# The second gated stage's down projection by pairs of batches, in seven block products instead of eight

## The chip, the cores and the metric

The kernel runs on one core of a Trainium2 chip. A core has a matrix engine (TensorE, PE in the rows; PEld is its weight load), a vector engine (VectorE, DVE), an activation engine (ScalarE, ACT), GpSimd (POOL) and a queue engine for transfers (SyncE, SP), and 16 DMA engines that all queues share. The metric is the device time of one execution in microseconds. The kernel before took 1463.2 us, the median of three runs (1461.71 to 1463.65).

## The reference

Three stages follow each other on 4608 tokens (8 batches of 576): an attention against 32 learned memory slots, a gated feed-forward layer (512 to 1536 to 512), and an ELU feed-forward layer (512 to 2048 to 512).

```
a = softmax(phi, axis=2);  k_m = a^T k;  v_m = a^T v          # per batch and head
attn = softmax(q k_m^T / 8) v_m                                # x, 4608 x 512
g = x @ w_gate;  val = x @ w_val
x = (g * sigmoid(g) * val) @ w_out                             # moe,  d_ff 1536
h = x @ w_in
out = where(h > 0, h, exp(min(h, 0)) - 1) @ w_out2             # moe2, d_ff 2048
```

The weights are float64, and a product of rounded 32-bit values would not be exact enough: every operand is kept as a high and a low part (`hi`, `lo`), and every product is three matmuls, hi*hi, hi*lo and lo*hi.

## The kernel before, in words

The 1536 hidden units of the gated layer are twelve blocks of 128, called `u`. The first four are computed right behind each batch's attention (the program's first part, to about 320 us); the other eight in a stage of their own (320 to about 763 us), which reads the attention weights `at` of each batch back from DRAM. The ELU layer is the last stage (756 us to the end). This case is about the middle stage.

In the middle stage the loop `for ps in range(2)` takes four `u` at a time, and inside it all eight batches and both halves of 288 tokens. `vw` folds the values of a batch into the gate and value weights, so that a gate tile is `up1` (line 213): six matmuls of 288 columns (L217, L218, L219). `gate1` ends in a SiLU on ScalarE (L238), `val2` in a product on VectorE (L571), which writes hidden values into token windows of 512 columns that do not agree with the batches of 576. When a window of a `u` is full, `split2h` makes its high part on ScalarE (L228) and its low part on VectorE (L230), and `down2` multiplies it by the four output blocks of `w_out`: twelve matmuls of 512 columns (L222 to L224). There are nine windows, eight `u` each: 72 times twelve, 864 matmuls. After four `u` ScalarE empties the four accumulators (L590), and a GpSimd DMA adds them to `p1d`, the layer's output in DRAM (L591).

Beside this runs `conv`, background work in small portions: the float64 weights are fetched (`wr`), split into words on ScalarE and VectorE (lines 114 to 119 and 132), and for the sixteen weight sets of the last stage `set_split` (L174) also makes the sums of weight blocks that the seven-product method needs, splits them and stores them (`upd`, `dnd`). The last stage already uses seven products for its pairs of token blocks; its first block of 512 tokens, the plain block, is done with eight.

The order of instructions on each engine is fixed when the program is built: a scheduler places them by its own estimate of times, by priorities (`tc.high_priority`) and by `tc.issue_after`. Each engine then takes its list in order. The pools (`wa`, `wo`, `hs` and so on) have a fixed number of buffers; a writer waits for the reader of the buffer's last content.

```
def split2h():
    w, u = chunks.pop(0)
    ready.append((w, u, split_h(hs_p, hw.pop((w, u)), T)))
def down(ps, w, hs, ms, start, stop):
    mm(ps, lhsT=w[0][:, ms], rhs=hs[0], start=start, stop=False)
    mm(ps, lhsT=w[1][:, ms], rhs=hs[0], start=False, stop=False)
    mm(ps, lhsT=w[0][:, ms], rhs=hs[1], start=False, stop=stop)
```

Of the kernel before, what the change touches and what calls it, by code (L numbers as in the profile page):

```python
# [29 lines left out]
NWA = 14  # L30
NWB = 4
# [6 lines left out]
def attention_moe_moe(ctx: ExitStack, tc: tile.TileContext, qT, phiT, kv, kv4, w1g, w1o, w2, out):  # L38
# [8 lines left out]
    wa_p = ctx.enter_context(tc.tile_pool(name="wa", bufs=NWA))  # L47
    st_l = ctx.enter_context(ExitStack())
    wr_p = st_l.enter_context(tc.tile_pool(name="wr", bufs=2))
    wt_p = st_l.enter_context(tc.tile_pool(name="wt", bufs=2))  # L50
    vx_p = st_l.enter_context(tc.tile_pool(name="vx", bufs=4))
    vt_p = st_l.enter_context(tc.tile_pool(name="vt", bufs=B))
# [7 lines left out]
    io_p = st_r.enter_context(tc.tile_pool(name="io", bufs=2, side="right"))  # L60
# [15 lines left out]
    up_d = [dram.tile([128, 8, 2, 256], F32, name=f"upd{q}") for q in range(NQD)]  # L76
    dn_d = [dram.tile([128, 8, 4, 2, 256], F32, name=f"dnd{h}") for h in range(2)]
# [86 lines left out]
    def store_w2():  # L164
        while stores:
            dst, w = stores.pop(0)
            nc.scalar.dma_start(out=dst, in_=w)

    def set_load(kind, q):
        t = SET[kind, q] = uq_p.tile([128, 8, 256], F32, tag="uq", name="uq")  # L170
        load_w(t[:, 2:6].rearrange("p r c -> p (r c)"), fetch_w(w2[q, :, int(kind == "down")]))

    def set_split(kind, q):
        t = SET.pop((kind, q))  # L174
        with later():
            tt(out=t[:, 0:7:6], in0=t[:, 4:6], in1=t[:, 2:5:2], op=ALU.subtract)
            tt(out=t[:, 1], in0=t[:, 5], in1=t[:, 0], op=ALU.subtract)
            tt(out=t[:, 7], in0=t[:, 3], in1=t[:, 1], op=ALU.subtract)
            for r in (0, 4):
                w = up_p.tile([128, 4, 2, 256], F32R, tag="u", name="uw")  # L180
                act(out=w[:, :, 0], in_=t[:, r:r + 4], func=AF.Copy)
                tt(out=w[:, :, 1], in0=t[:, r:r + 4], in1=w[:, :, 0].bitcast(F32), op=ALU.subtract)
                if kind == "up":
                    stores.append((up_d[q][:, r:r + 4], w.bitcast(F32)))
                else:
                    stores.append((dn_d[q // 4][:, r:r + 4, q % 4].rearrange("p r i c -> p r (i c)"),
                                   w.rearrange("p r i c -> p r (i c)").bitcast(F32)))
# [7 lines left out]
    def vw(b, p, pools):  # L195
        t = VW[b, p] = vx_p.tile([128, 2, 2, 512], F32R, tag="vx", name="vw")
        ps = [pool.tile([128, 512], F32, tag=tag, name="pvw") for pool, tag in pools]
# [23 lines left out]
    def down(ps, w, hs, ms, start, stop):  # L221
        mm(ps, lhsT=w[0][:, ms], rhs=hs[0], start=start, stop=False)  # L222
        mm(ps, lhsT=w[1][:, ms], rhs=hs[0], start=False, stop=False)  # L223
        mm(ps, lhsT=w[0][:, ms], rhs=hs[1], start=False, stop=stop)  # L224
# [255 lines left out]

    PD = [(ps_gv, "g")] * 2
    prev = []
    for b in range(B):
# [3 lines left out]
        if b == 0:  # L487
            wo = [lambda u=u: load_wo(u, wa_p) for u in range(UA // 2)]
# [3 lines left out]
        if 4 <= b <= 5:  # L492
            bk += [lambda: load_wg(2, b - 4, wa_p)]
        if b == B - 2:
            wb_p = st_l.enter_context(tc.tile_pool(name="wb", bufs=NWB))
# [6 lines left out]
            fr += [lambda: load_wg(3, 0, wa_p)]  # L502
        if b == B - 1:
            fr += [lambda: load_wg(3, 1, wa_p)]
            fr.append(lambda: load2(0))
            fr += [lambda: load_wo(2, wb_p)]
            fr += [lambda: vw(0, 2, G2)]
            fr += [lambda: load_wo(3, wb_p)]
            fr += [lambda: vw(0, 3, G2)]
# [44 lines left out]
    ps_acc = st_p2.enter_context(tc.tile_pool(name="ps_acc", bufs=1, space=PSUM))  # L554
    st_r = ExitStack()
    hs_p = st_r.enter_context(tc.tile_pool(name="hs", bufs=2, side="right"))
    p1_p = st_r.enter_context(tc.tile_pool(name="p1", bufs=1, side="right"))
    hw_p = st_r.enter_context(tc.tile_pool(name="hw", bufs=2 * UA, side="right"))
    t_p = st_r.enter_context(tc.tile_pool(name="t2", bufs=2, side="right"))
    up_p = st_l.enter_context(tc.tile_pool(name="up", bufs=3))  # L560
    uq_p = st_l.enter_context(tc.tile_pool(name="uq", bufs=1))

    hw, accs, chunks, ready = {}, {}, [], []

    def val2(b, hf, u, s):
        pv = ps_gv.tile([128, HS], F32, tag="g", name="pv")
        up1(pv, VW[b, u // 2], 256 * (u % 2) + 128, at2[b], HS * hf)
        for w, o, c0, c in windows(S * b + HS * hf, HS):
            if o == 0:
                hw[w, u] = hw_p.tile([128, T], F32, tag="h", name="h")  # L570
            last["h"] = stt(out=hw[w, u][:, o:o + c], in0=s[:, c0:c0 + c], scalar=1.0, in1=pv[:, c0:c0 + c],  # L571
                            op0=ALU.mult, op1=ALU.mult)
            if o + c == T:
                chunks.append((w, u))

    def split2h():
        w, u = chunks.pop(0)
        ready.append((w, u, split_h(hs_p, hw.pop((w, u)), T)))

    def down2():  # L580
        w, u, hs = ready.pop(0)
        first, last_u = u % UA == 0, u % UA == UA - 1
        if first:
            accs[w] = [ps_acc.tile([128, T], F32, tag=f"acc{m}", name=f"acc{m}") for m in range(KD)]
        for m in range(KD):
            down(accs[w][m], WO[u], hs, slice(128 * m, 128 * m + 128), first, last_u)
        if last_u:
            p1 = p1_p.tile([128, KD, T], F32, tag="p1", name="p1a")
            for m, acc in enumerate(accs.pop(w)):
                act(out=p1[:, m, :], in_=acc, func=AF.Copy)  # L590
            nc.gpsimd.dma_start(out=p1_d[w], in_=p1, accum_op=ALU.add)  # L591

    def turn():
        if chunks:
            split2h()
        if len(ready) > 1 or ready and not chunks:
            down2()
# [5 lines left out]
    def split_x(k):  # L603
        w = wa_p.tile([128, 2, T], F32R, tag="w", name="xs")
        with later(), tc.issue_after(last["gate"].ins):
# [6 lines left out]
    conv = [lambda p=p, k=k: load_wg(p, k, wa_p) for p in (4, 5) for k in range(2)] + \  # L612
        [lambda u=u: load_wo(u, wa_p) for u in (4, 5)] + \
        [lambda f=f, a=a: f(*a) for kind in ("up", "down") for q in range(NQD)
         for f, a in ((set_load, (kind, q)), (set_split, (kind, q)))]
    vwq = []
    slot, NCONV = 0, len(conv)
    for ps in range(2):
        for b in range(B):
            nb, np_ = (b + 1, ps) if b + 1 < B else (0, ps + 1)  # L620
            for hf in range(2):
                if hf == 0 and np_ < 2:
                    load2(nb)
                for u in range(UA * (ps + 1), UA * (ps + 2)):
                    s = gate1(b, u, at2[b], HS * hf, True)
                    val2(b, hf, u, s)
                    if slot * NB // (2 * B) < (slot + 1) * NB // (2 * B):
                        turn()
                    if vwq:
                        vw(*vwq.pop(0), V2)  # L630
# [4 lines left out]
                    if np_ == 2 and hf == 1:  # L635
                        split_x(u % UA)
# [293 lines left out]
```

## Time and profile before

| what | value |
|---|---|
| median of three runs | 1463.2 us |
| the profiled execution's own time | 1464.55 us |
| its span, first to last instruction | 1462.8 us |
| TensorE busy | 1433.3 us, 98% of the span |
| VectorE busy | 1073.0 us, 73% |
| ScalarE busy | 842.0 us, 58% |
| DMA, mean rate | 214 GB/s |

A busy TensorE here means that some matmul was in the array. Matmuls overlap in the array, so the duration of one (394 ns for 512 columns) is not what it costs: that is the distance between the starts of two, and it is read from the timeline. In the same way two VectorE instructions that do not depend on each other overlap a little. An engine that is not the bound costs nothing by being busy, until another one waits for it.

### The profile page before, as it was taken

The numbers are of one execution on the slowest core, as the hardware profiler recorded it, in microseconds if no ns is written. First come the engines' busy times: TensorE is split into PE (matmuls) and PEld (weight loads), VectorE is DVE, ScalarE is ACT, GpSimd is POOL, SyncE is SP. The second block draws the span as 40 slices with busy tenths as digits, with TensorE's granted clock in tenths as the row PEclk, the third lists the DMA queues.
The fourth block names the chain that finished last, engine by engine and source line by source line (L and its number), as shares of the span: only waits on it lengthen the run. The fifth ranks groups of instructions, "written<-read, shape, count | busy, mean of one in ns | idle before, by whom it ended". The sixth has DMA issues, their size and how long they took to land.

```text
span 1462.8 us, 22195 instructions
## 1 busy us (share of the span) xinstructions
PE 1433.3 (98%) x8782; PEld 1195.7 (82%) x8782; DVE 1073.0 (73%) x1500; ACT 842.0 (58%) x1296; POOL 36.9 (3%) x61
## 2 busy tenths in 40 slices
PE   5899999999999999999999999999999999999998
PEld 3678888998888888888888888888888888888887
DVE  7997777768866767777725548985889488957884
ACT  4665545544545545544537468655875498548842
POOL 0000000000000000000000000000000000000000
PEclk8999999999999999999999999999999999999999
DMA  9787523445676768876657765766675656666553
GB/s 379 292 294 255 180 93 107 140 159 177 205 220 226 244 224 235 248 217 216 211 170 221 251 211 189 272 212 200 199 263 210 221 192 239 237 227 198 198 208 130
DMA packets 72984, 313.39 MB, mean 214 GB/s; under 512 B 10289, under 2 KB 19505, under 8 KB 47921
## 3 DMA queue, kind: packets, MB, share of 16 engines
q1 hardware_dynamic: 42832, 240.67, 47.4%
q0 software_dynamic: 5472, 28.32, 8.8%
q10 hardware_dynamic: 24576, 43.00, 7.9%
q8 instruction: 69, 1.13, 0.3%
q14 instruction: 35, 0.28, 0.1%
HBM read 231.21 MB, written 80.74 MB: 213 GB/s over the span
## 4 chain that ended last, share of the span: by engine, by line
PE 89%; DMA 4%; DVE 3%; issue 2%; ACT 1%; POOL 0%; ACTq 0%; SPq 0%; POOLq 0%; DVEq 0%
PE pu L674 11%; PE pu L675 11%; PE pu L673 11%; PE acc L223 5%; PE acc L222 4%; PE acc L224 4%; PE pd L675 4%; PE pd L674 4%; PE pd L673 4%; PE pg L217 3%; PE pvw L201 3%; PE pv L217 3%; PE pg L219 3%; PE pv L219 3%; PE pv L218 3%; PE pg L218 3%
## 5 line engine op out<-in xcount | busy, mean ns | idle before, releaser
L674 PE MATMUL pu<-xlo,w 128*128 128x512 f32 x672 | 261.5, 389 | 0.0
L675 PE MATMUL pu<-xhi,w 128*128 128x512 f32 x672 | 261.5, 389 | 0.0
L673 PE MATMUL pu<-xhi,w 128*128 128x512 f32 x672 | 261.4, 389 | 0.0
L702 ACT ACTIVATE xhi<-g 128x1024 fp32r<-128x1024 f32 x120 | 126.6, 1058 | 108.6 <-PE pu L675 63.6
L703 DVE TENSOR_TENSOR xlo<-g,xhi 128x1024 fp32r<-128x1024 f32 x120 | 145.0, 1220 | 44.6 <-ACT xhi L702 44.5
L673 PEld LDWEIGHTS pu<-xhi,w 128*128 128x128 f32 x672 | 126.1, 188 | 26.4
L674 PEld LDWEIGHTS pu<-xlo,w 128*128 128x128 f32 x672 | 126.1, 188 | 26.2
L675 PEld LDWEIGHTS pu<-xhi,w 128*128 128x128 f32 x672 | 126.1, 188 | 26.1
L693 DVE SCALAR_TENSOR_TENSOR et<-et 128x1024 f32<-128x1024 f32 x72 | 87.8, 1220 | 53.6 <-ACT et L692 53.6
L228 ACT ACTIVATE hh<-h 128x512 fp32r<-128x512 f32 (+1 forms) x136 | 73.5, 541 | 92.7 <-DVE h L571 39.5
L571 DVE SCALAR_TENSOR_TENSOR h<-s,pv 128x288 f32<-128x288 f32 (+8 forms) x192 | 61.7, 349 | 88.4 <-PE pv L219 77.6
L217 PE MATMUL pg<-at,vw 128*128 128x288 f32 x384 | 118.8, 309 | 0.9 <-issue 0.4
L219 PE MATMUL pg<-at,vw 128*128 128x288 f32 x384 | 114.7, 299 | 1.3 <-DVE vw L210 1.3
L218 PE MATMUL pg<-at,vw 128*128 128x288 f32 x384 | 114.6, 298 | 1.2 <-DVE at L382 1.2
L217 PE MATMUL pv<-at,vw 128*128 128x288 f32 x384 | 115.1, 300 | 0.5 <-ACT s L238 0.4
L238 ACT ACTIVATE s<-pg 128x288 f32<-128x288 f32 x136 | 55.5, 410 | 104.1 <-PE pg L219 74.6
L218 PE MATMUL pv<-at,vw 128*128 128x288 f32 x384 | 113.7, 296 | 0.0
L219 PE MATMUL pv<-at,vw 128*128 128x288 f32 x384 | 113.4, 295 | 0.0
L223 PE MATMUL acc<-hh,wol 128*128 128x512 f32 x288 | 113.3, 394 | 0.0
L222 PE MATMUL acc<-hh,woh 128*128 128x512 f32 x288 | 113.1, 393 | 0.0
L673 PE MATMUL pd<-xhi,w 128*128 128x512 f32 x288 | 112.0, 389 | 0.0
L674 PE MATMUL pd<-xlo,w 128*128 128x512 f32 x288 | 112.0, 389 | 0.0
(133 smaller groups left out, 3150.0 us busy)
## 6 DMA issues: line engine op xcount, KB each, us to landing
w<-dnd SPq DMA_DIRECT2D x64, 1024.0 KB, 4.9
w<-upd SPq DMA_DIRECT2D x40, 1024.0 KB, 5.8
w<-upd SPq DMA_DIRECT2D x32, 768.0 KB, 4.7
at<-atd SPq DMA_DIRECT2D x16, 1152.0 KB, 6.0
p1d<-p1a POOLq DMA_DIRECT2D x18, 1024.0 KB, 8.4
kvr<-kv SPq DMA_DIRECT2D x32, 512.0 KB, 7.9
wr<-w SPq DMA_DIRECT2D x16, 1024.0 KB, 5.6
upd<-uw ACTq DMA_DIRECT2D x16, 1024.0 KB, 5.2
```

Source lines behind the costliest of these rows:

```text
L217: mm(ps, lhsT=wh, rhs=ah, start=g == 0, stop=False)
L218: mm(ps, lhsT=wh, rhs=al, start=False, stop=False)
L219: last["pe"] = mm(ps, lhsT=wl, rhs=ah, start=False, stop=g == 1)
L222: mm(ps, lhsT=w[0][:, ms], rhs=hs[0], start=start, stop=False)
L223: mm(ps, lhsT=w[1][:, ms], rhs=hs[0], start=False, stop=False)
L228: act(out=hh, in_=h, func=AF.Copy)
L673: mm(ps, lhsT=w[0], rhs=x[0], start=start, stop=False, skip_group_check=skip)
L674: mm(ps, lhsT=w[0], rhs=x[1], start=False, stop=False, skip_group_check=skip)
L675: last["mm"] = mm(ps, lhsT=w[1], rhs=x[0], start=False, stop=stop, skip_group_check=skip)
L693: stt(out=a, in0=e, scalar=1.0, in1=a, op0=ALU.add, op1=ALU.mult)
L702: last["hi"] = act(out=hi, in_=x, func=AF.Copy)
L703: last["lo"] = tt(out=lo, in0=x, in1=hi.bitcast(F32), op=ALU.subtract)
```

## The change

The middle stage is rewritten around pairs of batches. For a pair, all eight `u` are computed first, with a tile that holds both 288-halves (`up2`, `unit2`): 16 units of 24 matmuls. The hidden values of the pair stay in four tiles `gh`, by batch and by half of the `u`. Then `down_group` computes the pair's down projection as a 2 by 2 by 2 block product (batch, half of the `u`, half of the outputs) with seven products. Each product takes 48 matmuls of 288 columns: four pieces of operand (`hh` on ScalarE, L638; `hl` on VectorE, L639) times two weight tiles. The sums of hidden blocks are eight VectorE additions per pair of batches (L643); the sums of weight blocks are made once by `set_split` as a third kind of set ("first"), stored to `d1d` and fetched per product (`ws`, L633). A product's accumulators are emptied by ScalarE (L607) and added to one or two quarters of `p1d` by GpSimd DMAs (L610).

Around it: `load_wo` is left for the first four `u` alone; four "first" sets take its place, two of them in the program's first part; weight conversions of the gate and value weights move to earlier batches; two of the sixteen sets of the last stage move into its plain block (`rest`); the last stage's pools are placed anew, with six buffers of `o` become five, the weight tiles `w3` in the `vx` pool and the operands `S3`, `S4`, `A22` in other pools.

```
-NWA = 14
-NWB = 4
+NWA = 8
+NWO = 4
+NSET = (NU1 - UA) // 2
...
-            for r in (0, 4):
-                w = up_p.tile([128, 4, 2, 256], F32R, tag="u", name="uw")
...
+            for r in (2, 4, 0, 6):
+                store_w2()
+                w = up_p.tile([128, 2, 2, 256], F32R, tag="u", name="uw")
...
-        if 4 <= b <= 5:
-            bk += [lambda: load_wg(2, b - 4, wa_p)]
+        if 2 <= b <= 5:
+            bk += [lambda: load_wg(2 + (b - 2) // 2, b % 2, wa_p)]
...
+    turn = [3, 2] + [0, 1, 2] * (2 * NU1 * B)
+    def up2(b, u, c, name):
+        ps = bank2(turn.pop(0), name)
+        for hf in range(2):
+            up1(ps[:, hf, :HS], VW[b, u // 2], 256 * (u % 2) + c, at2[b], HS * hf)
+        return ps[:, :, :HS]
+    def unit2(b, u, out):
+        pg = up2(b, u, 0, "pg")
+        s = t_p.tile([128, 2, HS], F32, tag="s", name="s")
+        last["gate"] = act(out=s, in_=pg, func=AF.Silu)
+        pv = up2(b, u, 128, "pv")
+        last["h"] = stt(out=out, in0=s, scalar=1.0, in1=pv, op0=ALU.mult, op1=ALU.mult)
+    def add_part(banks, dst):
+        e = ev_p.tile([128, 2, S], F32, tag="e", name="ev")
+        for m in range(2):
+            act(out=e[:, m].rearrange("p (g s) -> p g s", g=2), in_=banks[m], func=AF.Copy)
+        for b, c in dst:
+            for w, o, c0, n in windows(S * b, S):
+                nc.gpsimd.dma_start(out=p1_d[w][:, 2 * c:2 * c + 2, o:o + n], in_=e[:, :, c0:c0 + n],
+                                    accum_op=ALU.add)
+    STEPS1 = [("P1", 2, 0, "D", [(0, 0)]), ("P4", 7, 3, "X", [(1, 0)]), ("P6", 1, 0, "D", [(0, 1)]),
+              ("P2", 3, 1, "X", [(0, 0)]), ("P7", 6, 3, "D", [(1, 0), (1, 1)]), ("P5", 0, 2, "X", [(1, 1)]),
+              ("P3", 5, 1, "X", [(0, 1)])]
+    def down_group(n, g):
...
+            if n < B // 2 - 1 and name == "P3":
+                for i, (b, p) in enumerate(pairs[8 * n + 8:8 * n + 10]):
+                    vw2(b, p, i)
+            for j in range(2):
+                w = wo_p.tile([128, 2, 2, 256], F32R, tag="w", name="ws")
+                last["ws"] = nc.sync.dma_start(out=w.bitcast(F32), in_=d1_d[:, r, 2 * j:2 * j + 2])
+                for hf in range(2):
+                    hs = [hs_p.tile([128, 2, HS], F32R, tag=t, name=t) for t in ("hh", "hl")]
+                    x = g[k][:, hf, 2 * j:2 * j + 2]
+                    with tc.high_priority():
+                        act(out=hs[0], in_=x, func=AF.Copy)
+                        last["h"] = last["gate"] = tt(out=hs[1], in0=x, in1=hs[0].bitcast(F32), op=ALU.subtract)
+                    if (name, 2 * j + hf) in COMB:
+                        o, a, b, f = COMB[name, 2 * j + hf]
+                        with tc.issue_after(last["h"].ins):
+                            tt(out=g[o][:, f], in0=g[a][:, f], in1=g[b][:, f],
+                               op=ALU.add if name == "P1" else ALU.subtract)
+                    for i in range(2):
+                        for m in range(2):
+                            down(acc[chain][m][:, hf], (w[:, i, 0], w[:, i, 1]), (hs[0][:, i], hs[1][:, i]),
+                                 slice(128 * m, 128 * m + 128), start and j + i == 0, j + i == 2, not start)
+                if name in (("P2", "P7", "P5", "P3") if n < 3 else ("P7", "P3")) and j == 0:
+                    background(late[n], len(late[n]) - 1)
+            add_part(acc[chain], [(2 * n + bi, c) for bi, c in dst])
```

The order on VectorE, in the middle of the second stage before: `h` is the product of gate and value, `hl` a low part for the down projection, `uq`, `uw` and `wc` the background weight set, `vw` the folded weights.

```order
L182 TENSOR_TENSOR uw<-uq,uw 128x4x256
L230 TENSOR_TENSOR hl<-h,hh 128x512
L182 TENSOR_TENSOR uw<-uq,uw 128x4x256
L210 TENSOR_TENSOR vw<-pvw,vw 128x512 x2
L571 SCALAR_TENSOR_TENSOR h<-s,pv 128x64
L571 SCALAR_TENSOR_TENSOR h<-s,pv 128x224
L230 TENSOR_TENSOR hl<-h,hh 128x512
```

And now, on VectorE at the start of the first pair's down block: `gh` are the pair's hidden values, L643 the sums of blocks.

```order
L597 SCALAR_TENSOR_TENSOR gh<-s,pv 128x2x288 x4
L643 TENSOR_TENSOR gh<-gh 128x1152 x2
L639 TENSOR_TENSOR hl<-gh,hh 128x576 x2
L643 TENSOR_TENSOR gh<-gh 128x1152
L639 TENSOR_TENSOR hl<-gh,hh 128x576
L643 TENSOR_TENSOR gh<-gh 128x1152
L639 TENSOR_TENSOR hl<-gh,hh 128x576 x4
L643 TENSOR_TENSOR gh<-gh 128x1152
L639 TENSOR_TENSOR hl<-gh,hh 128x576 x3
L643 TENSOR_TENSOR gh<-gh 128x1152
L118 TENSOR_SCALAR wc<-uq 128x1024
L639 TENSOR_TENSOR hl<-gh,hh 128x576
```

Low parts that were spread among the gate products now stand together, with the sums between them, and the background set follows from the fifth product on.

SyncE's queue in the same stage before, `at` the attention weights of a batch, `wr` a raw weight:

```order
L478 DMA at_4319<-atd_108 128x2304
L101 DMA wr<-w1g 128x2048
L478 DMA at_4528<-atd_109 128x2304
L101 DMA wr<-w1g 128x2048
L101 DMA wr<-w1o 128x2048 x2
L478 DMA at_4828<-atd_110 128x2304
```

And now, from before the first down block to behind it, `ws` a weight tile of a product:

```order
L633 DMA ws<-d1d 128x1024
L104 DMA wr<-w1o 128x2048
L104 DMA wr<-w1g 128x2048
L104 DMA wr<-w 128x2048 x2
L633 DMA ws<-d1d 128x1024 x2
L494 DMA at_4890<-atd_112 128x2304
L633 DMA ws<-d1d 128x1024
L494 DMA at_5009<-atd_113 128x2304
L633 DMA ws<-d1d 128x1024 x8
L104 DMA wr<-w 128x2048
```

Fourteen `ws` loads per pair of batches join the queue; the first four stand ahead of the second `at` load of the next pair, the others behind it.

## Rows read from the trace of the kernel before

**Rows 1.** The profile page: engines, granted clock by slice, the ending chain.
```profile
PE 1433.3 (98%) x8782; PEld 1195.7 (82%) x8782; DVE 1073.0 (73%) x1500; ACT 842.0 (58%) x1296; POOL 36.9 (3%) x61
...
PEclk8999999999999999999999999999999999999999
...
PE 89%; DMA 4%; DVE 3%; issue 2%; ACT 1%; POOL 0%; ACTq 0%; SPq 0%; POOLq 0%; DVEq 0%
```

**Rows 2.** Windows of stage two: busy PE, PEld, DVE, ACT, POOL; clock, DMA.
```profile
450.00:500.00 50.00, 49.24 (x319) 41.74 (x318) 36.34 (x61) 24.84 (x45) 2.35 (x2) 1.00 0.70 225
...
550.00:600.00 50.00, 50.00 (x337) 41.63 (x335) 37.21 (x64) 28.19 (x48) 1.53 (x2) 1.00 0.80 255
...
650.00:700.00 50.00, 48.97 (x319) 41.50 (x318) 33.55 (x58) 23.07 (x41) 1.75 (x3) 1.00 0.73 220
```

**Rows 3.** Timeline of PE, matmuls of 512 columns: start us, us, engine, line.
```profile
486.65 0.39 PE L222 MATMUL acc<-hh,woh 128*128 128x512 f32 x1
...
489.39 0.29 PE L217 MATMUL pv<-at,vw 128*128 128x288 f32 x1
```

**Rows 4.** The same, matmuls of 288 columns.
```profile
269.42 0.29 PE L222 MATMUL pd<-hh,woh 128*128 128x288 f32 x1
...
272.98 0.29 PE L217 MATMUL pg<-at,vw 128*128 128x288 f32 x1
```

**Rows 5.** Weight loads of stage two by shape: count, busy us, mean ns, idle.
```profile
L223 PEld LDWEIGHTS acc<-hh,wol 128*128 128x128 f32 x280 | 52.5, 188 | 11.6 <-issue 3.4
```

**Rows 6.** VectorE groups by shape, whole run: busy us, mean ns, idle before.
```profile
L210 DVE TENSOR_TENSOR vw<-pvw,vw 128x512 fp32r<-128x512 f32 x92 | 60.7, 683 | 13.3 <-ACT vw L205 13.1
...
L230 DVE TENSOR_TENSOR hl<-h,hh 128x512 fp32r<-128x512 f32 x72 | 49.4, 686 | 26.6 <-ACT hh L228 26.3 <-issue 0.2
...
L116 DVE SCALAR_TENSOR_TENSOR uq<-uq,wc 128x1024 int32<-128x1024 int32 x16 | 19.5, 1220 | 0.2
...
L382 DVE TENSOR_TENSOR at<-ex,at 128x576 fp32r<-128x576 f32 x16 | 11.9, 746 | 0.9 <-ACT at L381 0.8
...
L115 DVE TENSOR_SCALAR wc<-uq 128x1024 int32<-128x1024 int32 x16 | 11.0, 689 | 0.3 <-ACT uq L114 0.3
...
L286 DVE TENSOR_REDUCE nmx<-ph 128x2 f32<-128x1152 f32 x8 | 10.8, 1351 | 5.0 <-DMA ph<-phiT 5.0
...
L177 DVE TENSOR_TENSOR uq<-uq 128x256 f32<-128x256 f32 x16 | 6.8, 423 | 0.3
```

**Rows 7.** Timeline of VectorE: start us, us, line.
```profile
475.67 0.68 DVE L210 TENSOR_TENSOR vw<-pvw,vw 128x512 fp32r<-128x512 f32 x1
476.27 0.68 DVE L118 TENSOR_SCALAR wc<-uq 128x1024 int32<-128x1024 int32 x1
```

**Rows 8.** ScalarE groups by shape: busy us, mean ns, idle before.
```profile
L590 ACT ACTIVATE p1a<-acc 128x512 f32<-128x512 f32 x72 | 41.6, 598 | 16.1 <-PE acc L224 14.0
...
L114 ACT ACTIVATE uq<-wr 128x1024 f32<-128x1024 f32 x16 | 18.1, 1134 | 6.9 <-DVE h L571 3.4 <-DVE uw L182 3.4
...
L381 ACT ACTIVATE at<-ex 128x576 fp32r<-128x576 f32 x16 | 10.9, 684 | 4.4 <-DVE ex L379 2.5 <-PE pv L219 1.5 <-ACT s L241 0.5
```

**Rows 9.** DMA queues (packets, MB, share) and issues (KB, us to landing).
```profile
q1 hardware_dynamic: 42832, 240.67, 47.4%
q0 software_dynamic: 5472, 28.32, 8.8%
q10 hardware_dynamic: 24576, 43.00, 7.9%
...
w<-upd SPq DMA_DIRECT2D x32, 768.0 KB, 4.7
...
p1d<-p1a POOLq DMA_DIRECT2D x18, 1024.0 KB, 8.4
```

**Rows 10.** Waits of PE in stage two: us in total, times, longest.
```profile
PE pg L219 <- DVE vw L210: 1.3, 2, 0.9
```

**Rows 11.** Window of the third batch in the first part, as in rows 2.
```profile
106.00:136.00 30.00, 29.87 (x321) 25.65 (x321) 25.50 (x53) 16.13 (x42) 0.00 (x0) 1.00 0.72 234
```

More of the change, by code (lines that the diff above doesn't have):

```diff
@@ L559, in attention_moe_moe @@
+    hs_p = st_r.enter_context(tc.tile_pool(name="hs", bufs=4, side="right"))
     t_p = st_r.enter_context(tc.tile_pool(name="t2", bufs=2, side="right"))
[L560 to L597, printed above, removed]
+    gh_p = st_r.enter_context(tc.tile_pool(name="gh", bufs=4, side="right"))
+    def bank2(i, name):
+        return (ps_3 if i == 3 else ps_2).tile([128, 2, T], F32, tag=f"g{i}", name=name)
+    turn = [3, 2] + [0, 1, 2] * (2 * NU1 * B)
[4 more added lines that the diff above has]
+        return ps[:, :, :HS]
@@ L642, in attention_moe_moe, with sets @@
-    while chunks or ready:
-        turn()
+    def sets(kind, q):
+        return [lambda: set_load(kind, q), lambda: set_split(kind, q)]
+    todo = [(kind, q) for kind in ("up", "down") for q in range(NQD)]
+    conv = [[lambda: load_wg(5, 0, wa_p)] + sets("first", 2) + [lambda: load_wg(5, 1, wa_p)] +
+            sets("first", 3)]
+    late = []
+    for n in range(B // 2):
+        late.append([f for _ in range(2 - n // 3) for f in sets(*todo.pop(0))])
+        if n < B // 2 - 1:
+            conv.append([f for _ in range(2 + n // 2) for f in sets(*todo.pop(0))])
@@ new lines, in attention_moe_moe, with background @@
+    rest = [f for s in todo for f in sets(*s)]
+    def background(fs, x):
+        while fs and len(fs) > x:
+            fs.pop(0)()
+    pairs = [(2 * n + bi, UA // 2 * (k + 1) + j) for n in range(B // 2) for k in range(2) for bi in range(2)
+             for j in range(UA // 2)]
+    load2(1)
+    len0 = [len(c) for c in conv]
+    background(conv[0], len0[0] - 2)
+    for n in range(B // 2):
+        g = {}
+        slot = 0
+        for i, (b, p) in enumerate(pairs[8 * n:8 * n + 8]):
+            k = i // 2 % 2 * 2 + i // 4
+            if i % 2 == 0:
+                g[k] = gh_p.tile([128, 2, UA, HS], F32, tag="gh", name="gh")
+            for u in (2 * p, 2 * p + 1):
+                unit2(b, u, g[k][:, :, u % UA])
+                slot += 2
+                background(conv[n], len0[n] * (1 - slot / 24))
+            if n == B // 2 - 1:
+                if i == 0:
+                    fetch_x()
+                elif 4 <= i:
+                    split_x(i - 4)
+            if i < 6:
+                vw2(*pairs[8 * n + i + 2], 3)
+            if i in (5, 7) and n < B // 2 - 1:
+                load2(2 * n + 2 + i // 7)
+        down_group(n, g)
@@ L706, in g_tiles @@
     def g_tiles():
-        return [g_p.tile([128, 4, 2, T], F32, tag="g", name="g3") for _ in range(NQD // 2)]
+        return [p.tile([128, 4, 2, T], F32, tag="g", name="g3") for p in (g_p, g_p, gb_p, gb_p)]
     def store_out(t0, d, ps, engine, add=None):
@@ L755, in run_tasks, with run_rest @@
                 tasks.pop(0)[1]()
+    def run_rest(upto):
+        while rest and rest[0][0] <= upto:
+            with tc.high_priority():
+                rest.pop(0)[1]()
     def spread(tasks, first, last):
@@ L762, in attention_moe_moe @@
     xops = {}
-    todo = spread(x_tasks(T, xops), 0, 7)
-    G = g_tiles()
+    todo = spread(x_tasks(T, xops), 2, 7)
+    rest = spread(rest, -1, 4)
+    G = [t[:, i:i + 2] for t in (g_p.tile([128, 4, 2, T], F32, tag="g", name="g3") for _ in range(2)) for i in (0, 2)]
     for q in range(NQD):
-        w = fetch(up_d[q][:, 2:6])
+        with tc.issue_after(last["ws"].ins):
+            w = fetch(up_d[q][:, 2:6])
         ps = [bank((2 * q + i) % 6) for i in range(2)]
```

145 lines of the change are left out of this document (72 added, 73 removed).

## The prediction

> **What bounds the kernel now.** I read the page's engine line, its clock row and the chain of waits first [rows 1]: TensorE is busy for 98% of the span, the granted clock is at its upper level after the first slice, and TensorE holds 89% of the chain that ends last. So a change counts by the matmul time that it takes out, less the waits that it brings. The windows of the second stage say the same [rows 2]: of four times 50 us TensorE lacks 0.76 us and 1.03 us in two of them, VectorE has 11 to 17 us to spare in each and ScalarE over 20. The two gaps are waits for VectorE where background work stood ahead of a folded weight; two of them make 1.3 us [rows 10]. The DMA share is 0.70 to 0.80, the second fullest resource.
>
> What a matmul costs is the distance of starts on the timeline. Twelve matmuls of 512 columns lie between 486.65 and 489.39 us [rows 3], 0.2283 us each. Twenty-seven of 288 columns lie between 269.42 and 272.98 us [rows 4], 0.1319 us each.
>
> **TensorE, removed and added.** The old down projection is nine windows times eight `u` times twelve matmuls of 512 columns, 864 x 0.2283 = 197.3 us. The new one is four pairs times seven products times 48 matmuls of 288 columns, 1344 x 0.1319 = 177.2 us. The columns fall to seven eighths, but each matmul pays about 0.012 us beside its columns, and there are 480 more. Gates, folded weights and the last stage keep their counts. The balance is 20.1 us less, all of it on the path, because nothing else filled those stretches. The old stage's gaps, 1.8 us in rows 2, I also count as gone: a gate tile now holds both halves, so VectorE and ScalarE get twice the time before TensorE needs the bank again.
>
> One rule speaks against trading long matmuls for more short ones. A weight load takes 188 ns [rows 5], longer than the 0.132 us between short matmuls, and yet they follow each other at that distance [rows 4]: loads hide. The Trainium skill, page "TensorE: Matmul & The Clock Gate", section "The mechanism", says a load overlaps a running matmul only where the row groups differ; here all use all rows. With its load of 128 columns at about 107 ns (section "LDWEIGHTS") on top of every matmul, an estimate by that page would make the change some 29 us dearer. Rows 4 do not agree with it.
>
> **VectorE in a down block.** Low parts used to be spread over the stage; now a pair's 28 stand together, 28 x 0.746 = 20.9 us (L382 has the same 576 elements and types) [rows 6]. Eight sums of 1152 elements at 1.351 (L286, the only row of that length; a sum of two inputs is not in the trace, so by the 1.22 of 1024 elements, L116, it is 1.22 at least and twice the 0.746 at most) are 10.8. A weight set is two shifts and masks at 0.689, three operations at 1.22, five of 512 elements at 0.683 and two at 0.423, 9.3 us; the first three blocks have two, 18.6. Four parts of folded weights at 0.683 are 2.7. Together 53.0; the first product's four low parts stand ahead of the block, which leaves 50.0. Neighbours that do not depend on each other start 0.60 us apart where they take 0.68 [rows 7], so some 60 instructions give back 4.8: 45.2 us. TensorE has 336 x 0.1319 = 44.3, the next pair's first gate (1.6) and two foldings in it. That is almost level. What saves it is the order: ten of the second set's twelve instructions stand behind the last low part, about 6.5 us, and run on into the gate block, where VectorE has some 41 to 43 us of work in 16 x 24 x 0.1319 = 50.6 us. So low parts come in time on average, with four pieces of 12 x 0.1319 = 1.6 us as a cushion.
>
> **ScalarE.** 28 high parts at 0.684, fourteen evictions of as many elements, the sets and the foldings are about 36 us of 46 [rows 8]: no bound, but one joint. The sixth and the seventh product share their banks. Behind the two foldings TensorE has 20 matmuls and a gate, 4.3 us; in that time ScalarE owes four evictions of 0.598, a conversion of 1.134, a high part and the first bank's eviction, 4.9 us, plus handovers. I take 1 us for each of three joints (bounds 0 and 3), and 0.8 us for late low parts and bank changes in each of four blocks (bounds 0 and 2.5): 6 us of new waits.
>
> **Other parts.** The conversions of gate weights in earlier batches add 2 x 0.689 + 3 x 1.22 = 5.0 us to a batch in which VectorE is busy 25.50 of 30 us [rows 11]: 30.5 of 30, so 0.5 us there (bounds 0 and 2), with room in the next one. The two sets in the plain block: its first half asks VectorE for 8 x (1.22 + 2 x 0.683) = 20.7 and 18.6 us in 192 x 0.2283 = 43.8, so they hide; if they did not, 1 to 4 us. The last stage's rearranged pools change no count; I take nothing, and at most 5 us once where a pair block waits for memory that the last weight set leaves.
>
> **Sum.** 20.1 + 1.8 - 6 - 0.5 = 15.4 us. The profiled execution took 1464.55 us and would take 1449.2; it lies 1.35 us above the median, so the forecast for the median is 1463.2 - 15.4 = 1447.8, rounded to 1448 us. With no new waits at all it is 1441, with twice as many 1454.
>
> **Rivals.**
> *The DMA engines become the bound in the down blocks; slower.* By the queue rows [rows 9] a megabyte costs 2.88 us of all sixteen engines on SyncE's queue (47.4% of 1462.8 us for 240.67 MB), 4.54 on GpSimd's with its additions in DRAM, 2.69 on ScalarE's. A down block asks for fourteen `ws` of 0.52 MB (21.1 us), eight additions of 0.59 MB (21.4), two sets' stores of 4.2 MB (11.3) and two raw weights (6.0): 59.8 us in 46 to 48. If TensorE waited for all of it, three blocks would lose 12 us and the last 5, some 41 us: 1463.2 - 20 + 41 = 1484. It decides only once a `ws` takes longer than its lead, three tiles of 24 matmuls, 9.5 us. For it: additions of 1 MB took 8.4 us to land. Against it: weights of 768 KB took 4.7 us at shares like these, and additions and stores may drain in the gate block, which asks for about 27 us in 50; over a whole pair it is 87 of 97 us. Chance 9%.
>
> *VectorE becomes the bound there; less gain or slower.* Low parts waited 26.6 us in 72 for their high parts, 0.37 each [rows 6]. If all 28 of a block do, and nothing overlaps, 50.0 + 10.3 = 60 us stand against 48: 12 us a block, which would end at 1480; the gain is gone at 5 us a block. Against it: those waits in the old stage were idle time, with VectorE at 70%. Chance 11%, half of it between 1455 and no change.
>
> *The weight loads show after all.* If a short matmul could not start before its own 188 ns load had ended, 1344 x 0.188 = 252.7 us would replace 197.3: 1519 us. Rows 4 speak against it; 1%.
>
> *All of the new waits are hidden.* The scheduler has put gates of the next pair into the joints; then 1441 us. I leave it inside the forecast's own range, 1441 to 1455, which holds 75%; 4% is for something that I do not see.
>
> **Numbers.** What a measurement tells from no change is 0.2%, 2.9 us: faster means below 1460.3. The forecast and the near half of the VectorE case give faster 83%; 7% for no change; 10% for slower, most of it the DMA case. The range 1440 to 1459 leaves out the far ends of the two rivals and a little below.
>
> **What would show it.** In the profile after: 1344 matmuls `acc` of 288 columns at about 0.132 us, TensorE's busy time some 18 to 20 us lower, and in the second stage gaps of TensorE that sum to 4 to 9 us, at the seventh product's start and ahead of low parts. The forecast is wrong in its main term if short matmuls stand further apart in the down blocks than in rows 4, and wrong in its waits if weight loads are released by DMA of `ws`, or if VectorE is busy without a gap through the blocks while TensorE waits for `hl`.

## The result and the profile after

The changed kernel took **1474.6 us** (median of five runs, 1472.25 to 1479.73) against 1463.65 of the kernel before beside it: a ratio of 1.0081, 95% interval 1.0059 to 1.0104. It is slower, 27 us above the forecast of 1448 and outside its range. The profiled execution took 1472.25 us, the lowest of the five and 2.35 us under their median; its span is 1470.5.

The page of the changed kernel, busy time by engine and the granted clock by slice, answers to [rows 1].

```profile
PE 1417.7 (96%) x9262; PEld 1217.5 (83%) x9262; DVE 1144.5 (78%) x1500; ACT 864.9 (59%) x1300; POOL 98.8 (7%) x107
...
PEclk8999999999999999999998999999999999999999
```

TensorE is busy 15.6 us less than before, and yet the span is 7.7 us longer. So the matmul time went, and TensorE stands idle for more than it gained; one slice in the middle has lost clock. Windows over the middle stage and the plain block (columns as in [rows 2]: busy PE, PEld, DVE, ACT, POOL; clock, DMA share, GB/s) say where:

```profile
400.00:450.00 50.00, 46.74 (x380) 42.72 (x380) 41.32 (x58) 29.48 (x49) 14.71 (x12) 1.00 1.10 309
450.00:500.00 50.00, 50.00 (x406) 45.99 (x405) 37.14 (x52) 23.67 (x38) 2.13 (x2) 1.00 0.57 196
500.00:550.00 50.00, 46.69 (x373) 43.68 (x372) 41.35 (x57) 28.80 (x49) 17.49 (x15) 1.00 1.09 298
...
600.00:650.00 50.00, 44.77 (x340) 42.99 (x340) 40.68 (x52) 27.75 (x45) 14.71 (x12) 0.93 1.03 274
...
750.00:800.00 50.00, 39.98 (x185) 33.52 (x186) 21.43 (x28) 24.62 (x33) 5.17 (x5) 0.90 0.92 297
```

A gate block (450; 550 and 650 are alike) is as full as before; each of the first three down blocks (400, 500, 600) lacks 3 to 5 us and the plain block 10. The last down block (700 to 750), behind which no pair follows, lacks 0.3 us. VectorE has over 7 us to spare in each window shown, and 4.9 from 700 to 750, so it is not the bound. The DMA share is above 1.00 in the first three down blocks, where it was 0.70 to 0.80 [rows 2].

The waits of TensorE between 400 and 800 us (total, times, longest), and those of ScalarE for a DMA:

```profile
PE pu L735 <- DVE g L760: 9.7, 1, 9.7
PE pg L233 <- DVE vw L226: 8.1, 2, 5.2
PE pv L233 <- DVE vw L226: 2.9, 1, 2.9
```

```profile
ACT xhi L764 <- DMA p1d<-ev: 14.2, 1, 14.2
ACT uw L195 <- DMA upd<-uw: 7.9, 3, 3.9
ACT uw L195 <- DMA dnd<-uw: 7.3, 2, 6.2
```

There are four gaps: one in the plain block, and one at each joint, where a pair's last product meets the next pair's first unit (its gate `pg`, at the second joint its value `pv`). TensorE names VectorE each time; VectorE had waited for ScalarE, and ScalarE for a DMA: a store at the joints, an addition in the plain block. ScalarE's timeline at the first joint (start, us, engine, line; in brackets the idle time before):

```profile
414.67 1.05 ACTq L170 DMA_DIRECT2D upd<-uw  x2
...
416.80 0.61 ACT L195 ACTIVATE uw<-uq 128x512 fp32r<-128x512 f32 x1
417.95 0.60 ACT L221 ACTIVATE vw<-pvw 128x512 fp32r<-128x512 f32 x1 [0.54 <-PE pvw L217]
422.40 0.63 ACT L195 ACTIVATE uw<-uq 128x512 fp32r<-128x512 f32 x1 [3.85 <-DMA upd<-uw]
```

A weight set is converted in four pieces `uw`, but there are three buffers. The scheduler put the fourth piece between the evictions of the folded weights (L221). It waits until the first piece's store, issued at 414.67, has landed at about 422.3, 7.6 us later. The next two evictions stand behind it (422.93), and with them the next pair's folded weights. TensorE's timeline there and at the third joint:

```profile
421.27 0.29 PE L240 MATMUL acc<-hl,ws 128*128 128x288 f32 x1
424.41 0.40 PE L233 MATMUL pg<-at,vw 128*128 128x288 f32 x1 [2.85 <-DVE vw L226]
...
638.81 0.29 PE L240 MATMUL acc<-hl,ws 128*128 128x288 f32 x1
644.33 0.61 PE L233 MATMUL pg<-at,vw 128*128 128x288 f32 x1 [5.23 <-DVE vw L226]
...
645.22 0.44 PE L233 MATMUL pg<-at,vw 128*128 128x288 f32 x1
645.46 0.44 PE L234 MATMUL pg<-at,vw 128*128 128x288 f32 x1
```

Between starts lie 3.14 and 5.52 us instead of 0.13: gaps of 3.0 and 5.4 us (the second joint's is 3.0 too). Behind the third, matmuls follow each other at 0.24 us, the lower clock level (granted clock 0.50 from 644.3 to 648.2 us).

In the plain block, ScalarE, GpSimd and then TensorE:

```profile
776.25 0.60 ACT L752 ACTIVATE et<-pu 128x512 f32<-128x512 f32 x1
791.09 2.00 ACT L764 ACTIVATE xhi<-g 128x1024 fp32r<-128x1024 f32 x2 [14.24 <-DMA p1d<-ev]
```

```profile
779.62 1.21 POOL L610 DMA_DIRECT2D p1d<-ev  x1 [5.91 <-DVE uq L135]
```

```profile
783.99 0.39 PE L737 MATMUL pu<-xs,w 128*128 128x512 f32 x1
794.06 0.79 PE L735 MATMUL pu<-xs,w 128*128 128x512 f32 x1 [9.68 <-DVE g L760]
794.65 0.63 PE L736 MATMUL pu<-xs,w 128*128 128x512 f32 x1
795.08 0.63 PE L737 MATMUL pu<-xs,w 128*128 128x512 f32 x1
```

`xhi` takes its memory from the pool `op`, which now lies where the evicted accumulators `ev` were. Its first writer waits until the last addition out of `ev` has landed; GpSimd issued that one only at 779.62, having waited 12.3 us for an earlier addition to land and then the 5.9 us of the row, which names an instruction of the background set on VectorE; why an addition should wait for that stays open. The evictions `et`, which TensorE's banks need, stand behind `xhi` in ScalarE's list. TensorE loses 9.8 us, and then runs at 0.43 us per matmul of 512 columns until 798 (granted clock 0.50).

Queues and issues (columns as in [rows 9]) show why the stores are slow:

```profile
q0 software_dynamic: 20288, 28.32, 9.9%
...
ws<-d1d SPq DMA_DIRECT2D x56, 512.0 KB, 6.5
...
p1d<-ev POOLq DMA_DIRECT2D x8, 512.0 KB, 11.7
...
p1d<-ev POOLq DMA_DIRECT2D x8, 128.0 KB, 9.1
```

The same 28.32 MB of GpSimd's queue, 18.9 MB of additions and 9.4 MB of stores of the output, now make 20288 packets instead of 5472; an addition of 128 KB takes 9.1 us to land and one of 512 KB 11.7, where 1 MB took 8.4 before [rows 9].

### The profile page after: what moved, and what is told of

It is laid out like the page before. It is cut to its first block, busy times and chain, and to the rows that moved or that the text cites. A ratio compares the mean times of both kernels' runs of the same rounds, so it can differ in the third digit from the quotient of the medians.

```text
span 1470.5 us, 23383 instructions
## 1 busy us (share of the span) xinstructions
PE 1417.7 (96%) x9262; PEld 1217.5 (83%) x9262; DVE 1144.5 (78%) x1500; ACT 864.9 (59%) x1300; POOL 98.8 (7%) x107
## 3 DMA queue, kind: packets, MB, share of 16 engines
q0 software_dynamic: 20288, 28.32, 9.9%
## 4 chain that ended last, share of the span: by engine, by line
issue 48%; PE 38%; DMA 6%; DVE 5%; ACT 2%; POOL 2%; ACTq 0%; SPq 0%; POOLq 0%; DVEq 0%
PE acc L238 4%; PE acc L240 4%; PE acc L239 3%; PE pg L233 3%; PE pg L235 3%; PE pv L233 3%; PE pg L234 3%; PE pv L235 3%; PE pv L234 3%; PE pvw L217 3%; PE pd L238 2%; PE pd L240 2%; PE pd L239 2%; DMA wr<-w1g 2%; DMA dnd<-uw 1%
## 5 line engine op out<-in xcount | busy, mean ns | idle before, releaser
L238 PE MATMUL acc<-hh,ws 128*128 128x288 f32 x448 | 130.7, 296 | 1.2 <-ACT ev L607 1.2
L239 PE MATMUL acc<-hh,ws 128*128 128x288 f32 x448 | 130.6, 295 | 0.0
L610 POOL DMA_DIRECT2D p1d<-ev x64 | 78.5, 1589 | 700.9 <-DVE gh L643 388.0
L240 PE MATMUL acc<-hl,ws 128*128 128x288 f32 x448 | 123.9, 296 | 0.0
L735 PE MATMUL pd<-xhi,w 128*128 128x512 f32 x288 | 112.0, 389 | 0.0
L737 PE MATMUL pd<-xhi,w 128*128 128x512 f32 x288 | 112.0, 389 | 0.0
```

What stands on the lines that cost most here:

```text
L238: mm(ps, lhsT=w[0][:, ms], rhs=hs[0], start=start, stop=False, skip_group_check=skip)
L239: mm(ps, lhsT=w[1][:, ms], rhs=hs[0], start=False, stop=False, skip_group_check=skip)
L240: mm(ps, lhsT=w[0][:, ms], rhs=hs[1], start=False, stop=stop, skip_group_check=skip)
L735: mm(ps, lhsT=w[0], rhs=x[0], start=start, stop=False, skip_group_check=skip)
L737: last["mm"] = mm(ps, lhsT=w[1], rhs=x[0], start=False, stop=stop, skip_group_check=skip)
```

## The experiments

Two causes were put to the test: at the joints, a background piece in ScalarE's list that waits for a store; in the plain block, a pool that takes over memory from which a transfer still reads. The rival to both: the DMA engines are simply full, and TensorE waits for their throughput whatever stands where.

**Late piece.** The fourth piece of the first background set goes behind the evictions of the joint, and the second set behind it.

```
-            for r in (2, 4, 0, 6):
+          for r in rs:
...
+                    if n < 3 and name == "P5":
+                        continue
+                    if n < 3 and name == "P3":
+                        with tc.issue_after(last["ev"].ins):
+                            background(late[n], len(late[n]) - 1)
+                        background(late[n], 0)
```

> One edit: in the first three down blocks the fourth piece of the background weight set, which waits on ScalarE for a store to land, is issued behind the evictions of the sixth product instead of between those of the two foldings (the second set's load moves behind it too). Theory (ScalarE's list is blocked at the joint by that one wait): the three gaps of TensorE of 3.0, 3.0 and 5.4 us before the next pair's first gate go to under 1 us each, and the slow clock behind the third goes with it; about 1463 us against 1474.6, the plain block's gap of 9.8 us stays. Rival (the DMA engines are simply full in the down blocks, share 1.1, and another instruction will wait for them): the gaps move to another wait, the sum of TensorE's gaps in the second stage falls by less than 4 us, 1471 us or more.

Measured: 1463.98 us, ratio to before 1.0011 (1.0000 to 1.0022), 10.6 us under the changed kernel. TensorE's waits between 400 and 800 us:

```profile
PE pu L746 <- DVE g L771: 9.8, 1, 9.8
PE pg L234 <- DVE gh L598: 4.9, 5, 1.4
```

No wait for folded weights is left; the plain block's stays. New are five small waits inside the gate blocks.

**Pool order.** `op` is opened behind `wx` and `o3` and so gets other memory.

```
-    op_p = ctx.enter_context(tc.tile_pool(name="op", bufs=3, side="right"))
     wx_p = ctx.enter_context(tc.tile_pool(name="wx", bufs=2, side="right"))
     o3_p = ctx.enter_context(tc.tile_pool(name="o3", bufs=5, side="right"))
+    op_p = ctx.enter_context(tc.tile_pool(name="op", bufs=3, side="right"))
```

> One edit: of the last stage's pools on the right side, the high and low operands (op) are opened behind wx and o3, so that they no longer lie where the second stage's ev buffers were. Theory (the first high part of the plain block's down loop stands early in ScalarE's list and waits for the additions in DRAM that still read ev, 14.2 us): the gap of 9.8 us in the plain block and the 10 us of half clock behind it go, about 1463 us. Rival (the plain block waits for the additions themselves, or for its two weight sets, whatever lies over ev): the gap stays within 2 us, 1472 us or more.

Measured: 1463.27 us, ratio 1.0004 (0.9994 to 1.0013), 11.3 us under the changed kernel. Where ScalarE had waited 14.2 us it now waits 0.7, and not for a DMA:

```profile
770.69 1.06 ACT L764 ACTIVATE xhi<-g 128x1024 fp32r<-128x1024 f32 x1 [0.71 <-DVE g L760]
```

**Both together.**

> Both edits of the two other runs together. If the two gaps are independent, the gains add: about 1451 to 1453 us, faster than the kernel before (1463.6) by 11 us or so, and TensorE's gaps in the second stage and the plain block sum to what the forecast had (4 to 9 us over the foldings' own). If both come from one cause (full DMA engines), the sum falls short: over 1458 us.

Measured: 1452.67 us, ratio 0.9941 (0.9918 to 0.9965): faster than before by 0.6%. The gains add, 10.6 + 11.3 = 21.9 us, which is what the two kernels differ by. Its windows:

```profile
400.00:450.00 50.00, 50.00 (x413) 46.11 (x419) 44.08 (x61) 29.80 (x50) 14.71 (x12) 1.00 1.07 298
...
600.00:650.00 50.00, 50.00 (x403) 47.45 (x402) 42.26 (x55) 28.84 (x47) 15.92 (x13) 1.00 1.07 291
750.00:800.00 50.00, 50.00 (x223) 41.38 (x222) 37.75 (x49) 36.72 (x47) 3.75 (x3) 1.00 1.03 335
```

TensorE is busy throughout these windows with the DMA share as high as in the changed kernel. So full DMA engines alone do not make the four gaps: it is where a wait for them stands. What is left are waits for `gh` in the gate blocks, 4.0 us in three between 400 and 800 us.

**No addition**, in the changed kernel.

```
-                nc.gpsimd.dma_start(out=p1_d[w][:, 2 * c:2 * c + 2, o:o + n], in_=e[:, :, c0:c0 + n],
-                                    accum_op=ALU.add)
+                nc.gpsimd.dma_start(out=p1_d[w][:, 2 * c:2 * c + 2, o:o + n], in_=e[:, :, c0:c0 + n])
```

> The changed kernel with the DMAs of the second stage storing instead of adding, so that the partial products overwrite each other (the output is not the reference's). Pieces, sizes, queues and order stay. If the reading and writing back of the additions is what makes stores land late and the last additions end late: the store that ScalarE waits for lands in 4 to 5 us instead of 7.6, the gaps at the joints shrink to under 1.5 us, the plain block's gap to under 4 us, about 1460 us. If it is the number of small pieces and their chain of waits: landing times of the pieces stay near 11 us, 1471 us or more.

Measured: 1454.22 us, ratio 0.9936 (0.9922 to 0.9951), better than expected by 6 us. The joints shrink to 2.0, 1.7 and 0.7 us and the plain block's gap goes: with plain stores most transfers land earlier (medians: `ws` 4.8 us, `upd` 4.6; `dnd` 6.8 as before). The store for which ScalarE waits at the first joint still took 6.6 us, not 4 to 5, so this gap shrank least. So the slow landing and the place of the wait are both needed; taking away either one cures most of it.

**Store at once**: a piece's store ahead of the next piece.

```
-                store_w2()
+                store_w2(0)
```

> The changed kernel with one word different: each piece of a background weight set is stored before the next piece is converted, and not one piece later. In the changed kernel the first two stores of a set were issued together at 414.67 us, 3.1 us behind the end of the two conversions (411.57 us). Theory (at each joint ScalarE stands in front of a buffer whose store has not landed): stores leave some 2 to 3 us earlier, so the three gaps of 3.0, 3.0 and 5.4 us become about 0.3, 0.3 and 2.7, in all 7 to 8 us less; the plain block's 9.8 us stays; about 1467 us. Rival (the DMA engines are full, and it is their throughput that TensorE waits for, however early a store is issued): the gaps stay within 1 us of their size, 1473 to 1475 us.

Measured: 1473.95 us, ratio 1.0076 (1.0063 to 1.0089); the three gaps stay (8.5 us for `pg` and 2.4 for `pv`). This decides nothing, because the edit did not do what it was for: in the trace both stores still leave together, at 414.34 us, 0.06 us behind the start of the same conversion `hh` as in the changed kernel. The scheduler had left them where they were.

**Both, without addition.**

> Late piece and pool order together (1452.67 us), and in addition the quarters of the layer's output are stored plainly instead of added to what DRAM holds; the output therefore lacks the layer's other parts. Theory (slow additions cost time only through ScalarE's and the pool's waits, which the two edits have taken off TensorE's path): no change beyond 0.2% against the two edits alone, 1450 to 1454 us. Rival (full DMA engines still cost TensorE time in the down blocks): 1444 to 1448 us.

Measured: 1447.45 us, ratio 0.9895 (0.9881 to 0.9908), 5.2 us under both edits: the rival's figure, so the two edits had not taken everything off. ScalarE's waits for stores of weight pieces between 400 and 800 us, with the additions and then without:

```profile
ACT uw L196 <- DMA dnd<-uw: 9.1, 6, 4.0
ACT uw L196 <- DMA upd<-uw: 8.4, 5, 2.6
```

```profile
ACT uw L196 <- DMA dnd<-uw: 4.0, 5, 1.6
ACT uw L196 <- DMA upd<-uw: 3.6, 5, 1.7
```

TensorE's wait for `gh` falls from 4.0 us to 0.4 with them. The fourth piece also waits inside the gate blocks, in front of a gate's SiLU; there it costs 1 to 2 us at a time. These waits are not the whole of the 5.2 us: between 330 and 750 us TensorE's idle time falls from 6.5 to 3.8 us. The rest is not accounted for, and a kernel that moves those pieces alone was not run.

**Both, weights later**, by one batch.

```
-        if 2 <= b <= 5:
-            bk += [lambda: load_wg(2 + (b - 2) // 2, b % 2, wa_p)]
+        if 3 <= b <= 6:
+            bk += [lambda: load_wg(2 + (b - 3) // 2, (b - 3) % 2, wa_p)]
```

> Late piece and pool order together (1452.67 us), with the four early conversions of gate and value weights one batch later each, in batches 3 to 6 instead of 2 to 5. Theory (the gap of 0.9 to 1.6 us at 150 us is VectorE's, from the conversion in the batch where it is fullest): that gap goes to 0.3 us or less; batch 6, where now a weight set of the middle stage is made too, has room for it: 1451 to 1452 us. Rival (the work only moves its wait to batch 6 or 7): the gap goes and one of 0.5 to 2 us comes between 250 and 325 us, 1452 to 1454 us.

Measured: 1453.39 us, ratio 0.9934 (0.9921 to 0.9948): no gain. The gap at 150 us went, and waits of 0.8, 0.6, 0.4 and 1.6 us came between 185 and 324 us. The rival was right.

**Three parts, fourth buffer.** To take the wait away and leave the piece where it is, the fourth piece gets a buffer of its own; the memory comes from a buffer pair of `hs`. The control has only the latter.

```
-    hs_p = st_r.enter_context(tc.tile_pool(name="hs", bufs=4, side="right"))
+    hs_p = st_r.enter_context(tc.tile_pool(name="hs", bufs=3, side="right"))
...
+    UX.append(st_r.enter_context(tc.tile_pool(name="ux", bufs=1, side="right")))
...
-                w = up_p.tile([128, 2, 2, 256], F32R, tag="u", name="uw")
+                p = UX[0] if UX and r == 6 else up_p
+                w = p.tile([128, 2, 2, 256], F32R, tag="u", name="uw")
```

> Control for the next three: the changed kernel with three buffers instead of four for the high and low parts of the down blocks, which frees the memory that the next kernels use. Three pairs of parts are still a lead of 36 matmuls, 4.8 us. All theories: joints and plain block as in the changed kernel, 1472 to 1477 us; at most 3 us more where a low part comes late.

> The control with one buffer more: the fourth piece of a background weight set, in the middle stage, has a buffer of its own, so that it never waits for the store of the first piece. It still stands between the two foldings in ScalarE's list, and as many bytes go to DRAM. Theory (ScalarE's list stands at that buffer): the joint gaps of 3.0, 3.0 and 5.4 us fall to 1 us or less each, the half clock behind the third goes, and small waits in the gate blocks go too; 9 to 14 us less than the control, 1460 to 1465 us; the plain block's gap stays. Rival (the full DMA engines delay something else that TensorE needs there, a weight tile or an eviction): the gaps stay, same as the control.

Measured: the control 1476.83 us, ratio 1.0098 (1.0083 to 1.0113); with the fourth buffer 1468.27, ratio 1.0039 (1.0027 to 1.0052), 8.6 us less. The control's time was expected, its gaps were not. With three pairs of parts the scheduler made another order, in which TensorE stands at the joints for 1.7, 1.5 and 4.7 us in front of an accumulator's eviction `ev`, and for 4.4 us in the gate block behind the third. TensorE's waits in it between 320 and 850 us, apart from the plain block's:

```profile
PE acc L238 <- ACT ev L607: 8.1, 4, 4.6
PE pv L233 <- ACT s L595: 4.5, 2, 4.2
```

ScalarE's wait for a store in front of the fourth piece is there all the same, 2.6, 2.4 and 5.1 us at the three joints. So the 8.6 us are a comparison of two lists that differ in order too; the place of the fourth piece is to be compared with the changed kernel. With the fourth buffer, at the first joint the fourth piece (`uw`) still stands between the evictions of folded weights, and waits for nothing:

```profile
415.63 0.58 ACT L223 ACTIVATE vw<-pvw 128x512 fp32r<-128x512 f32 x1
...
416.76 0.61 ACT L197 ACTIVATE uw<-uq 128x512 fp32r<-128x512 f32 x1
...
417.80 1.09 ACT L223 ACTIVATE vw<-pvw 128x512 fp32r<-128x512 f32 x2 [0.42 <-DVE vw L228]
```

The first joint has no gap, the second one of 0.7 us. At the third, the second set still brings 2.9 and 3.2 us (649 and 655 us), where a piece waits 4.8 us for a store, and lower clock behind them; hence 8.6 us and not 9 to 14. The plain block's gap stays at 8.8 us. As many bytes go to DRAM, and the piece stands between the same two evictions as in the changed kernel: at the joints the wait for the buffer is the cause.

**Fourth buffer and pool order; and the late piece with them.** No new edits.

> The fourth buffer and the pool order together, nothing moved in any list on purpose. Theory: both waits go, and the gate blocks' waits for landed stores too, which the late piece left: 1447 to 1452 us, at or a little under the 1452.67 of late piece and pool order. Rival (waits for landed stores do not matter in the gate blocks): 1452 to 1455 us.

> Fourth buffer, late piece and pool order together. Theory: with a buffer of its own the late piece has nothing left to avoid, so no change against the fourth buffer and the pool order, within 2 us, 1447 to 1452 us. Rival (the place of the piece matters beside its buffer): 3 us or more below that one.

Measured: 1468.03 us, ratio 1.0042 (1.0029 to 1.0054), and 1468.81, ratio 1.0041 (1.0028 to 1.0055). Their likeness was expected, their level was not: the pool order, worth 11.3 us above, did nothing. VectorE in the first of them says why:

```profile
767.23 0.69 DVE L198 TENSOR_TENSOR uw<-uq,uw 128x512 fp32r<-128x512 f32 x1 [2.85 <-ACT uw L197]
777.55 1.28 DVE L764 TENSOR_TENSOR g<-et,pu 128x512 f32<-128x512 f32 x2 [9.63 <-DMA dnd<-uw]
```

Now `g` lies where the new buffer was, and waits for the last store out of that. TensorE stands for 9.0 us; only the name of the transfer is another. With the fourth buffer alone `g` had waited for it already, 10.0 us.

**Fourth buffer given back** ahead of the last down block, in both kernels.

```
+        if n == B // 2 - 1:
+            UX.clear()
         down_group(n, g)
-    UX.clear()
     st_r.close()
```

> Fourth buffer and pool order (1468.03 us), with the fourth buffer given up ahead of the last down block, whose one weight set takes its four pieces from the three old buffers. In the kernel with fourth buffer and pool order VectorE's first write of the plain block's g waited 9.6 us for a store of a weight piece: g lies where the fourth buffer was, and its last store landed at 777.5 us. Theory (the plain block waits for whatever transfer last uses the memory that its pools take over): the 9.0 us gap and the half clock behind it go, 1452 to 1456 us. Rival (the wait is for full DMA engines and finds another tile): a gap of 5 us or more stays in the plain block, 1460 us or more.

> Fourth buffer, late piece and pool order (1468.81 us), with the same early return of the fourth buffer. Theory: the 9.9 us gap and its half clock go, 1450 to 1456 us, and with it the comparison with late piece and pool order (1452.67 us, four buffers of parts) shows what the fourth buffer adds: within 3 us of that. Rival: a gap stays in the plain block, 1460 us or more.

Measured: 1456.49 us, ratio 0.9958 (0.9943 to 0.9972), and 1455.26, ratio 0.9944 (0.9931 to 0.9957). The gap is gone in both; between 400 and 800 us TensorE waits in the first of them only here for more than 0.6 us:

```profile
PE pv L235 <- ACT s L598: 2.4, 1, 2.4
PE pg L235 <- DVE gh L600: 2.4, 1, 2.4
```

So the plain block's gap follows the last transfer out of memory that the new pools take over, in three arrangements. The fourth buffer with three pairs of parts is no better than late piece and pool order with four, whose 1452.67 us is the best of the kernels that compute the whole reference.

## Why the prediction was wrong, point by point

- **TensorE, 20.1 us less: right.** Short matmuls stand 0.13 us apart in the down blocks too (below), 1344 of them, and busy time fell by 15.6 us although it now holds 3.7 us of lower clock.

```profile
410.43 0.30 PE L240 MATMUL acc<-hl,ws 128*128 128x288 f32 x1
410.56 0.29 PE L238 MATMUL acc<-hh,ws 128*128 128x288 f32 x1
```

- **Weight loads show, 1%: excluded rightly.** Loads of 188 ns follow each other under these matmuls. The sentence in the Trainium skill, page "TensorE: Matmul & The Clock Gate", section "The mechanism", that a load overlaps only where row groups differ, is not borne out by this spacing. The same section of the Trainium skill also names loads into the background weight buffer as pulled ahead of running matmuls. The prediction left that out, and the spacing of 0.13 us does not speak against it.
- **"I take 1 us for each of three joints (bounds 0 and 3)": this step failed.** The joints cost 3.0, 3.0 and 5.4 us, and some 1.7 us of lower clock behind the third (3.9 us at 0.24 instead of 0.13 us a matmul): 13 us where 3 were taken. The step added up the durations of what ScalarE had to do, 4.9 us against 4.3, as if none of it could wait for a DMA. Its terms are evictions, one raw weight's conversion (the 1.134 us of L114 [rows 8]) and a high part; the two pieces `uw` of 0.6 us that stand among them in the trace are not in it. The second of these waited for a store, 3.9, 3.9 and 6.2 us. The fourth buffer showed that this wait was the cause, the late piece what its place in the list costs.
- **"I take nothing, and at most 5 us once where a pair block waits for memory": this step failed too.** The mechanism was named, its place and price were wrong: not a pair block but the plain block, 9.8 us, and 2.0 us of lower clock behind it (4.3 us at 0.43 instead of 0.23). I asked what the last weight set leaves and not which transfer leaves the old pools last. The two steps together cost 24.9 us where 3 were taken, 22 of the 27 us (of the profiled execution, in which they are measured, 1449.2 us were expected and 1472.25 came: 21.9 of 23.1). Late piece and pool order gave 21.9 us back, less than the 24.9, since waits for `gh` came in their place; that 21.9 is also the excess over the 3 us taken is chance.
- **The other new waits, 0.8 us a block: a little high.** The bank changes cost 0.6 us in each of the first two blocks, none in the third and 0.5 in the last (with the joints the step makes 6.2 us, which the sum has as 6). Not foreseen were the waits for stores in the gate blocks, which the joints' edits uncovered: TensorE waits 4.0 us for `gh` there, most of the 5 us between both edits (1452.67) and the forecast.
- **Weight conversions in the first part, 0.5 us: too low.** TensorE waited 1.3 us for `p` of ScalarE at 150 us in the changed kernel; a batch later it is no better, so the first part as a whole had less room than that one window [rows 11] showed.
- **The DMA rival: wrong in its path, right in its cause.** It asked whether `ws` comes late; `ws` took 6.5 us (median) of its 9.5, 11.5 at most, and no wait of TensorE for it is in the list. Its 4.54 us a megabyte mixes additions with the output's plain stores on the same queue. But the overfull engines (59.8 us asked in 46 to 48, and indeed a share of 1.03 to 1.10) made stores and additions land late, and those were waited for. Its 9% should have counted every wait for a DMA in the lists of ScalarE, VectorE and GpSimd.
- **The VectorE rival: rightly small.** VectorE has 7 us or more to spare in the windows shown and 4.9 in the last down block, and TensorE waited for no low part. (In the old stage it had 13 to 17 us to spare by [rows 2], not 11.)
- **All waits hidden, 1441 us: not reached.** Without additions and with both edits 1447.45 us is the best that was seen.

## What to carry to other kernels

An engine's list between two deadlines is not the sum of its instructions' durations: go through it and ask of each whether it writes a buffer from which a transfer still reads, when that transfer was issued, and how long such transfers take to land at the DMA load that the change itself brings. Background work with one buffer fewer than pieces does no harm where nothing urgent stands behind its last piece; where a scheduler put that piece ahead of an urgent one, it cost TensorE 3.0 to 5.4 us here. At a change of stage, write down for each new pool what lay in its memory and which transfer leaves it last; moving one pool only helps if its new neighbour is free earlier.

## What the runs showed of the hardware

A smaller addition into DRAM hardly lands sooner: 9.1 us for 128 KB and 11.7 us for 512 KB in the changed kernel; 1 MB took 8.4 us before, at a lower DMA share. GpSimd's queue moved 28.32 MB in both kernels, 18.9 MB of additions and 9.4 MB of output stores. Its packets took 9.9% of sixteen engines' 1470.5 us; with plain stores in place of the additions, in fewer packets, 5.1% of 1445.3 (the row below), about half. If the output's stores cost the same in both, the difference of 71.9 us falls to the 18.9 MB: by this estimate an addition takes 3.8 us of all sixteen engines per megabyte more than a plain store.

```profile
q0 software_dynamic: 8256, 28.32, 5.1%
```

In the changed kernel the granted clock was at the lower level behind the gaps of 5.4 and 9.8 us, and not behind the two of 3.0 us. The length of a gap alone does not order this: with both edits it fell behind a gap of 2.0 us (0.63 from 653 to 656 us).
